# Linear attention and gated feed-forward on one core: where the output stage's sums and residual adds run

## The chip, the cores and the metric

The kernel runs on one core of one Trainium2 chip. A core has a matrix engine (TensorE, PE, with its weight load PEld), VectorE (DVE), ScalarE (ACT), GpSimd (POOL) and a queue that issues transfers (SyncE, SP). Engines run their own instruction streams in order and meet through semaphores. The metric is the device time of one execution in microseconds, as the median of several runs.

## The reference

One token block of 2048 x 1024 (bf16) goes through a linear-attention layer and a gated feed-forward layer, each behind a layer norm and with a residual:

```python
qkv = (x @ wqkv) ...                       # x: layernorm(A_x), 32 heads of 32
phi = lambda t: jnp.where(t > 0, t + 1, jnp.exp(t)) + 1e-6
kv = jnp.einsum("bhsd,bhse->bhde", phi(k), v)
z = jnp.einsum("bhsd->bhd", phi(k))
o = num / den                              # num = phi(q) kv, den = phi(q) z + 1e-6
h = x + o @ wo
gate, up = n @ W_gate, n @ W_up            # n: layernorm(h), F = 3584
out = h + (relu(gate) * up) @ W_down
```

## The kernel before

The 2048 tokens are 16 tiles `st` of 128. Most products are done in a seven-product form (P1 to P7) of a 2 x 2 block product instead of eight: it needs sums of weight blocks (`TW`) and of operand blocks (`S`), made ahead of the products, and additions to the results.

The program is a plan written out by hand: `PL.add` puts an operation at the end of its engine's list, and waits follow from what each operation reads and writes. So the order of the calls in the source is the order on each engine, SP's queue included. Buffers that share memory are named in `over` lists; the first write of the new one waits for the readers of the old.

The stages around the change, in order:

- *Query stage.* `q_group(r, ct)` runs eight groups of seven products, with hooks 1 to 7 between the products. VectorE forms phi with an add (L1170), a fast SBUF clamp (L915) and a combination (L918). In the second half (`r = 1`), `a2_num` and `a2_div` of the first tiles run too: `a2_num` is 32 small products into banks 0 to 3, and `a2_div` on VectorE divides (L1306, L1309, L1311, giving `o_st`) and sends the tile through a transposing transfer on SP (`T3d_st`) into one of six `oT` slots.
- *Single tiles.* For tiles 0 to 9, `a4_mm(st)` multiplies `oT(st)` by `wo` with 16 products into a bank pair, (4, 5) or (6, 7). `a4_h(st)` adds the residual tile `x2(st)` on VectorE (L1460; tile 9 in two halves, L1333) into one of three `hsb` slots and stores it. For tiles 0 to 7 ScalarE then takes statistics and normalizes (`a4_norm`), and a transposing transfer `T5d_st` puts the tile into `hnT`. Calls of `a2_num`/`a2_div` for the following tiles are put between the products by the table `at`; the table `aft` puts other work behind a tile.
- *Weight sums of wo.* `wo_sums` makes TWo1 to TWo4 on GpSimd in halves (two blocks of 512), the first two before tile 0, the others behind tiles 0 to 5.
- *Grouped tiles.* Tiles 10 to 15 go in three pairs through `o_group(p, ...)`, p = 5, 6, 7, of seven products each. `o_sums(p, i)` makes the four operand sums So of a pair: one on GpSimd, eleven on VectorE (L1363). ScalarE copies banks (`ofk1`, `ofk2`, `os7`, `osc`); the residual is added by GpSimd (`add_x`, L1406) to the copies, and VectorE adds the parts (L1412) or, in the third group, bank and residual (L1419). `store` sends a tile out through SP.
- *Feed-forward.* It starts with unit 0 on `hnT` (P1 of two blocks, banks 1 and 0, copied by ScalarE to banks 4 and 5). It needs the operand sums S1 to S4 (`s_sums`, L1544, VectorE), the weight sums of its first weights (`t_sums`, L1568; for this unit on GpSimd as eight 128x512 pieces, `pool_t`), and inner sums xs and g1 (L1624, L1602, VectorE).

Memory that matters: region RA holds the transposed input until the query stage ends, then the TWo sums (8 K columns), the So sums (4 K), and four residual tiles `x2a` (12 to 15). `xn` in region RXH (4 K) holds normalized tiles. `x2r` in region RE has three slots for residual tiles 8 to 10, and tile 11 reuses the first of them.

Of the kernel before, what the change touches and what calls it, by code (L numbers as in the profile page):

```python
# [132 lines left out]
def bass_sequential_preLN__linear_attn_block__glu_gated_reglu__prompt_kernel(  # L133
# [71 lines left out]
    with es:  # L205
# [21 lines left out]
        NX2 = 3  # L227
        NDIR = 10
        NXA = NST - TPP - NX2 - 1
# [59 lines left out]
        TWo = RA[:, 0:NDC * D].bitcast(f16).rearrange("p (j k c) -> p j k c", j=4, k=KH)  # L289
        So = RA[:, NDC * D:(NDC + 4) * D].bitcast(f16).rearrange("p (z i k t) -> p z i k t", z=2, i=4, k=KH)  # L290
        x2a = RA[:, (NDC + 4) * D:(NDC + 4 + NXA) * D].rearrange("p (a b) -> p a b", a=NXA)
        NXR = TPP + NX2 + 1

# [39 lines left out]
        xn = RXH[:, 0:NXN * D].rearrange("p (a b) -> p a b", a=NXN)  # L333
        hsb = RXH[:, NXN * D:(NXN + NHS) * D].rearrange("p (a b) -> p a b", a=NHS)
# [106 lines left out]
        B_TWo = bufs("TWo_", 4)  # L441
        B_Ef = bufs("Ef_", 2)
# [73 lines left out]
        ra_o = B_TWo + flat(B_So) + B_x2[TPP + NX2:]  # L516
        for b_ in ra_o:
            b_.over = flat(B_xnT)
        for b_ in B_x2[0:TPP]:
            b_.over = B_TWk  # L520
# [26 lines left out]
        for i, st in enumerate(range(NDIR, NST)):  # L547
            if i < NHS:
                j = st % NHS
                hp_home[st] = hsb[:, j, :]  # L550
                over = [B_hs[j]]
            else:
                hp_home[st] = xn[:, i - NHS, :]
                over = [B_xn[i - NHS]]
            for b_ in B_hp[st]:
                b_.over = over
        for b_ in B_D1:
            b_.over = B_xn + B_hs + [b for st in B_hp for b in B_hp[st]]
# [18 lines left out]
        for b_ in flat(B_hh) + B_out2:  # L577
            b_.over = flat(B_xnT) + flat(B_pqT) + ra_o
# [743 lines left out]
        def a4_mm(st, at):  # L1322
            k = st % NOT
            b = a4_bank[st] = min(H_PAIRS, key=lambda b: max(bank_last[b], bank_last[b + 1]))
            for nt in range(ND2):
                touch_bank(b + nt)
                for ct in range(NG):
                    for f_ in at.pop(nt * NG + ct, ()):
                        f_()
                    mm(bank(b + nt, NW), oT(st)[:, ct, :], wo[:, ct, nt * NW:(nt + 1) * NW],  # L1330
                       ct == 0, ct == NG - 1, [B_oT[k], B_wo[nt]], B_bank[b + nt], "a4_%d_%d" % (st, nt))
                if st == NDIR - 1:
                    PL.add("dve", lambda e, h=slice(nt * NW, (nt + 1) * NW), bk=b + nt: e.tensor_tensor(  # L1333
                        out=hsb[:, st % NHS, h], in0=bank(bk), in1=x2(st)[:, h], op=ALU.add),
                        reads=[B_bank[b + nt], B_x2[x2_slot(st)]], writes=[B_hs[st % NHS]], name="h_%d_%d" % (st, nt))

        def wo_sums(j, eng, k0, k1):
# [3 lines left out]
            def t(i):  # L1341
                return TWo[:, i, k0:k1, :], [B_TWo[i]]
# [4 lines left out]
                   reads=x[1] + y[1], writes=[B_TWo[j]], name="TWo%d" % (j + 1))  # L1347
# [18 lines left out]
        def o_group(p, bks, hooks, act_first):  # L1366
# [3 lines left out]
            s7, sc = (btmp[:, 1, :], B_bt[1]), (btmp[:, 0, :], B_bt[0])  # L1370
# [11 lines left out]
            def TW(j):  # L1382
                return (lambda kk: TWo[:, j, kk, :]), [B_TWo[j]]
# [16 lines left out]
            def res(st, h):  # L1400
                return x2(st)[:, h * NW:(h + 1) * NW], B_x2[x2_slot(st)]

            def add_x(src, st, h, dst=None):
                x, bx = res(st, h)
                d, db = src if dst is None else dst
                PL.add("pool", lambda e: e.tensor_tensor(out=d, in0=src[0], in1=x, op=ALU.add),  # L1406
                       reads=[bx] + ([] if dst is None else [src[1]]), writes=[db], name="ox_%d_%d" % (st, h))

            def fin(st, h, bk, s=None):
                d, db = half(st, h)  # L1410
                if s is not None:
                    PL.add("dve", lambda e: e.tensor_tensor(out=d, in0=bank(bk), in1=s[0], op=ALU.add),  # L1412
                           reads=[B_bank[bk], s[1]], writes=[db], name="h_%d_%d" % (st, h))
                elif act_first:
                    ident_act(Ef[:, h, :], bank(bk), [B_bank[bk]], [B_Ef[h]], "oc_%d_%d" % (st, h))
                    add_x((Ef[:, h, :], B_Ef[h]), st, h, (d, db))
                else:
                    x, bx = res(st, h)
                    PL.add("dve", lambda e: e.tensor_tensor(out=d, in0=bank(bk), in1=x, op=ALU.add),  # L1419
                           reads=[B_bank[bk], bx], writes=[db], name="h_%d_%d" % (st, h))  # L1420
# [5 lines left out]

            prod(a, X(0, 0), W(0, 0), True, "P1")
# [3 lines left out]
            ident_act(s7[0], bank(f), [B_bank[f]], [s7[1]], "os7")  # L1431
            add_x(s7, sb2, 0)
            hook(2)
            prod(b, SX(1), TW(1), False, "P6")
            ident_act(bank(c), bank(b), [B_bank[b]], [B_bank[c]], "ofk2")
            hook(3)
            prod(a, X(1, 0), W(1, 0), False, "P2")
            fin(sa, 0, a)
# [3 lines left out]
            add_x(sc, sb2, 1)  # L1442
            hook(5)
            prod(b, X(1, 1), TW(3), False, "P4")
            fin(sb2, 0, b, s7)
            hook(6)
            fin(sb2, 1, f, sc)
            store(sb2)
            prod(c, SX(3), W(1, 1), False, "P3")
            o_pend[1] = [lambda: fin(sa, 1, c), lambda: store(sa)]  # L1450
# [4 lines left out]
        def a4_h(st):  # L1455
# [3 lines left out]
            if st < NDIR - 1:  # L1459
# [3 lines left out]
            if TPP <= st and st + NX2 < NST:  # L1463
                if st + NX2 < NXR:
                    load_x2(st + NX2)
# [1175 lines left out]
```

## Time and profile before

| what | us |
|---|---|
| median of 3 runs (lowest, highest) | 722.0 (721.59, 722.17) |
| the profiled execution's own time | 722.16 |
| its span in the trace | 720.4 |
| PE busy | 703.7 (98%) |
| VectorE busy | 615.3 (85%) |
| ScalarE busy | 413.0 (57%) |
| GpSimd busy | 143.0 (20%) |
| DMA, 16 engines, queue q1 | 66.5% of the span |

The times in the trace are microseconds from the start of its span; durations are busy times of single instructions. A matmul row carries several products; one 128x512 product takes about 0.22 us, four of them 0.87. Idle time in front of an instruction is given with what released it, for example a DVE line or a transfer. Where a wait was for several things, the trace names the last.

### The profile page before, as it was taken

The numbers are of one execution on the slowest core, as the hardware profiler recorded it, in microseconds if no ns is written. First come the engines' busy times: TensorE is split into PE (matmuls) and PEld (weight loads), VectorE is DVE, ScalarE is ACT, GpSimd is POOL, SyncE is SP. The second block draws the span as 40 slices with busy tenths as digits, with TensorE's granted clock in tenths as the row PEclk, the third lists the DMA queues.
The fourth block names the chain that finished last, engine by engine and source line by source line (L and its number), as shares of the span: only waits on it lengthen the run. The fifth ranks groups of instructions, "written<-read, shape, count | busy, mean of one in ns | idle before, by whom it ended". The sixth has DMA issues, their size and how long they took to land.

```text
span 720.4 us, 13204 instructions
## 1 busy us (share of the span) xinstructions
PE 703.7 (98%) x4984; PEld 392.3 (54%) x5039; DVE 615.3 (85%) x978; ACT 413.0 (57%) x745; POOL 143.0 (20%) x197
## 2 busy tenths in 40 slices
PE   8999999999898999999999999999999999999998
PEld 4434444444443444555554568875555555547887
DVE  6978867899888889999999787878898888988885
ACT  4977667764853668787877402036766666643010
POOL 3221100004878322132313002220000000000331
PEclk9999999999999999999999999999999999999999
DMA  9852344015997799999997999995443534267996
GB/s 300 255 105 73 44 133 161 2 30 97 218 186 219 243 319 313 306 268 293 274 296 223 261 276 300 306 267 135 117 132 103 160 92 137 87 195 249 317 326 186
DMA packets 195104, 144.21 MB, mean 200 GB/s; under 512 B 53984, under 2 KB 172512, under 8 KB 195040
## 3 DMA queue, kind: packets, MB, share of 16 engines
q1 hardware_dynamic: 190048, 138.77, 66.5%
q0 software_dynamic: 4032, 3.67, 3.6%
q8 instruction: 40, 0.66, 0.4%
q10 hardware_dynamic: 960, 0.92, 0.4%
q14 instruction: 24, 0.20, 0.1%
HBM read 98.76 MB, written 32.51 MB: 182 GB/s over the span
## 4 chain that ended last, share of the span: by engine, by line
PE 81%; DVE 11%; issue 3%; DMA 2%; POOL 2%; ACT 1%; SPq 0%; DVEq 0%; POOLq 0%
PE ps L831 81%; DVE RE L1311 1%; DVE RX L915 1%; DVE RAB L918 1%; DVE RO L1568 1%; DMA RE<-RE 1%; POOL RX L1406 1%; DVE RW L767 1%; DMA RAB<-RXH 1%; DVE RXH L1460 1%; DVE RC L1054 0%; DVE RAB L1702 0%; POOL RXH L1406 0%; DMA RAB<-in_A_x_dram 0%; DVE rden L1309 0%
## 5 line engine op out<-in xcount | busy, mean ns | idle before, releaser
L836 ACT ACTIVATE ps<-ps 128x512 f32<-128x512 f32 (+1 forms) x263 | 133.0, 517 | 181.2 <-PE ps L831 127.9
L831 PE MATMUL ps<-RC,RO 128*128 128x512 f16 x616 | 147.0, 369 | 0.0
L831 PEld LDWEIGHTS ps<-RC,RO 128*128 128x128 f16 x616 | 60.1, 98 | 53.1 <-ACT ps L836 1.4
L836 ACT ACTIVATE RE<-ps 128x512 f32<-128x512 f32 (+3 forms) x106 | 63.8, 627 | 30.9 <-PE ps L831 16.6
L831 PE MATMUL ps<-RC,RWG 128*128 128x512 f16 x320 | 80.8, 379 | 0.0
L831 PE MATMUL ps<-RH,RWG 128*128 128x512 bf16 (+1 forms) x347 | 77.6, 348 | 0.8 <-ACT ps L836 0.7
L1972 POOL DMA_DIRECT2D out_dram<-RX x20 | 17.9, 1232 | 271.2 <-DVE RX L1963 218.4
L831 PE MATMUL ps<-RAB 128*128 128x512 bf16 (+3 forms) x272 | 58.8, 352 | 3.0 <-DVE RE L1311 1.5
L831 PE MATMUL ps<-RH,RO 128*128 128x512 bf16 (+1 forms) x228 | 59.2, 379 | 1.5
L1702 DVE TENSOR_TENSOR RE<-ps,RE 128x1024 bf16<-128x1024 f32 (+1 forms) x42 | 44.0, 1047 | 18.0 <-PE ps L831 17.8
L831 PE MATMUL ps<-RW,RAB 128*128 128x256 f16 (+3 forms) x368 | 55.2, 302 | 1.1 <-ACT RX L836 0.8
L831 PEld LDWEIGHTS ps<-RH,RWG 128*128 128x128 bf16 x348 | 33.9, 98 | 36.2 <-ACT ps L836 1.4
L831 PEld LDWEIGHTS ps<-RC,RWG 128*128 128x128 bf16 (+1 forms) x320 | 30.0, 98 | 34.5 <-ACT ps L836 5.8
L831 PEld LDWEIGHTS ps<-RW,RAB 128*128 128x128 f16 (+1 forms) x374 | 36.4, 98 | 16.9 <-ACT RX L836 1.5
L1963 DVE TENSOR_TENSOR RE<-ps,RE 128x512 f32<-128x512 f32 x44 | 30.2, 686 | 14.4 <-PE ps L831 11.8
L836 ACT ACTIVATE RX<-ps 128x512 f32<-128x512 f32 (+1 forms) x47 | 27.5, 597 | 25.6 <-PE ps L831 20.5
L831 PEld LDWEIGHTS ps<-RAB 128*128 128x128 bf16 (+1 forms) x274 | 26.0, 98 | 28.3 <-ACT ps L836 3.2
L1714 ACT ACTIVATE RAB<-RAB 128x1024 bf16<-128x1024 bf16 x28 | 29.5, 1053 | 19.3 <-DVE RAB L1702 19.3
L1702 DVE TENSOR_TENSOR RAB<-ps,RE 128x1024 bf16<-128x1024 f32 x28 | 34.2, 1221 | 7.3 <-PE ps L831 4.6
L1702 DVE TENSOR_TENSOR RAB<-RAB,RE 128x1024 bf16<-128x1024 bf16 x56 | 37.2, 685 | 3.1 <-ACT RE L836 2.7
L1568 DVE TENSOR_TENSOR RO<-RWG 128x1024 f16<-128x1024 bf16 x54 | 39.4, 730 | 0.0
L831 PEld LDWEIGHTS ps<-RH,RO 128*128 128x128 f16 (+1 forms) x256 | 24.4, 98 | 24.6 <-ACT RX L836 1.5
(210 smaller groups left out, 1305.2 us busy)
## 6 DMA issues: line engine op xcount, KB each, us to landing
RWG<-in_B_W_gate_dram SPq DMA_DIRECT2D x28, 512.0 KB, 6.1
RWG<-in_B_W_up_dram SPq DMA_DIRECT2D x28, 512.0 KB, 5.0
RW<-l_scr SPq DMA_DIRECT2D x20, 448.0 KB, 5.9
RW<-in_B_W_down_dram SPq DMA_DIRECT2D x14, 512.0 KB, 6.4
t_scr<-RW SPq DMA_DIRECT2D x14, 512.0 KB, 4.2
l_scr<-RX SPq DMA_DIRECT2D x7, 1024.0 KB, 8.5
RE<-l_scr SPq DMA_DIRECT2D x15, 448.0 KB, 6.1
RW<-t_scr SPq DMA_DIRECT2D x13, 448.0 KB, 5.7
```

The source lines that it names most:

```text
L767: PL.add("dve", lambda e: e.tensor_tensor(out=out, in0=in0, in1=in1, op=ALU.subtract), reads=reads, writes=writes, name="WT_%d" % q)
L831: lambda e: e.matmul(out_ap, lhsT, rhs, start=start, stop=stop, skip_group_check=skip),
L836: PL.add("act", lambda e: e.activation(out=dst, in_=src, func=func), reads=reads, writes=writes, name=name)
L915: PL.add("dve", lambda e: e.tensor_scalar(out=Et[:, k, :], in0=Et[:, k, :], scalar1=1.0, scalar2=1e-6, op0=ALU.min, op1=ALU.add), reads=[] ...
L918: PL.add("dve", lambda e: e.scalar_tensor_tensor(out=dst_ap, in0=src, scalar=C1, in1=Et[:, k, :], op0=ALU.add, op1=ALU.max), reads=[src_bu ...
L1311: PL.add("dve", lambda e: e.tensor_tensor(out=osb[:, k, :].rearrange("p (g h e) -> p g h e", h=HPG, e=Dh), in0=nv[:, :, :, 0:Dh], in1=rden ...
L1406: PL.add("pool", lambda e: e.tensor_tensor(out=d, in0=src[0], in1=x, op=ALU.add), reads=[bx] + ([] if dst is None else [src[1]]), writes=[ ...
L1568: PL.add(eng, lambda e: e.tensor_tensor(out=tb(j, u), in0=f0(u), in1=f1(u), op=ALU.subtract), reads=[B_w[i + x] for x in r] + ([B_T[k + x] ...
L1702: PL.add("dve", lambda e: e.tensor_tensor(out=dst, in0=in0, in1=in1, op=op), reads=reads, writes=writes, name=name)
L1714: PL.add("act", lambda e: e.activation(out=d, in_=d, func=ACTF.Relu), reads=[], writes=db, name=name)
L1963: PL.add(eng, lambda e: e.tensor_tensor(out=dst, in0=in0, in1=in1, op=op), reads=reads, writes=writes, name=name)
L1972: PL.add("pool", lambda e: e.dma_start(dst, src, accum_op=ALU.add), reads=[bsrc], writes=[B_hscr[st]], slot=sl, name="acc_%d_%d" % (st, dh))
```

## The change

The output stage divides its work otherwise between VectorE, GpSimd and ScalarE.

- All twelve So sums are made by GpSimd; GpSimd no longer adds residuals.
- In `o_group`, VectorE adds the residual as it reads the bank: `os7` and `ofx` (bank f plus each half of tile `sb2`'s residual, into SBUF as fp32), the two halves of tile `sa` from their banks, `hp` (the copy `osc` plus `ofx`, both in SBUF) and the last half from its bank. The ScalarE copies `os7` and `oc` are gone.
- TWo3 and TWo1 are made in the query stage, one 512 block in each of its eight groups, at hook 5, each waiting for the operation before the last one planned on VectorE. TWo2 and TWo4 stay behind tiles 2 to 5. TWo1 and TWo3 live in `xn`'s place; the normalized tiles move to `xo` in RA.
- For tiles 8 and 9 ScalarE writes the residual into the bank pair before the products (`a4_pre`), the products add to it, and ScalarE copies the sum out in halves. `a4_pre` also chooses the bank pair of every single tile.
- `x2r` has four slots; tile 11's residual is loaded with the others instead of after tile 8.
- The places in `at`, `aft` and the groups' hooks change: the divisions of tiles 12 to 15 come earlier, T5d_5 to T5d_7 later, the loads of residual tiles 12 to 15 earlier, and the S sums are spread over the third group.
- The first writes of the feed-forward tiles wait only for what lies in their own place in RA.

```diff
-        NX2 = 3
+        NX2 = 4
...
+        def TWo(j):
+            return (TWo_x if j % 2 == 0 else TWo_a)[:, j // 2]
...
-            b = a4_bank[st] = min(H_PAIRS, key=lambda b: max(bank_last[b], bank_last[b + 1]))
+            b, pre = a4_bank[st], st >= TPP
...
-                       ct == 0, ct == NG - 1, [B_oT[k], B_wo[nt]], B_bank[b + nt], "a4_%d_%d" % (st, nt))
-                if st == NDIR - 1:
-                    PL.add("dve", lambda e, h=slice(nt * NW, (nt + 1) * NW), bk=b + nt: e.tensor_tensor(
-                        out=hsb[:, st % NHS, h], in0=bank(bk), in1=x2(st)[:, h], op=ALU.add),
...
+                       ct == 0 and not pre, ct == NG - 1, [B_oT[k], B_wo[nt]], B_bank[b + nt], "a4_%d_%d" % (st, nt),
+                       skip=pre)
+                if pre:
+                    hs, h = st % NHS, slice(nt * NW, (nt + 1) * NW)
+                    ident_act(hsb[:, hs, h], bank(b + nt), [B_bank[b + nt]], [B_hs[hs]], "h_%d_%d" % (st, nt))
+
+        def a4_pre(st):
+            b = a4_bank[st] = H_PAIRS[st % 2]
+            if st >= TPP:
+                ident_act(ps[:, b:b + 2, :], x2(st).rearrange("p (a c) -> p a c", a=2), [B_x2[x2_slot(st)]],
+                          [B_bank[b], B_bank[b + 1]], "hx_%d" % st)
...
             prod(f, SX(2), TW(2), True, "P7")
-            ident_act(s7[0], bank(f), [B_bank[f]], [s7[1]], "os7")
-            add_x(s7, sb2, 0)
+            fin(s7, f, res(sb2, 0), "os7_%d" % p)
...
             ident_act(bank(c), bank(b), [B_bank[b]], [B_bank[c]], "ofk2")
+            fin(fx, f, res(sb2, 1), "ofx_%d" % p)
...
-            fin(sa, 0, a)
+            fin(half(sa, 0), a, res(sa, 0), "h_%d_0" % sa)
...
-            add_x(sc, sb2, 1)
+            fin(half(sb2, 1), [sc[0], [sc[1]]], (fx[0], [fx[1]]), "hp_%d_1" % sb2, fin_eng)
             hook(5)
             prod(b, X(1, 1), TW(3), False, "P4")
-            fin(sb2, 0, b, s7)
+            fin(half(sb2, 0), b, (s7[0], [s7[1]]), "h_%d_0" % sb2)
+            store(sb2)
...
+                hooks[5] = lambda i=r * (NG // 2) + ct: wo_sums((2, 0)[i // KH], "pool", i % KH, i % KH + 1,
+                                                               PL.prog["dve"][-2:-1])
...
-              6: {5: [nd]}, 7: {3: [nd]}, 8: {2: [nd, t5(4)]}, 9: {2: [nd, t5(5)]}}
-        aft = {0: [tw(2, 0)], 1: [tw(2, 2)], 2: [tw(1, 0)], 3: [tw(1, 2)], 4: [tw(3, 0)], 5: [tw(3, 2)],
-               8: sums(p0, (2, "pool")), 9: sums(p0, (0, "dve"), (1, "dve"), (3, "dve"))}
+              6: {5: [nd]}, 7: {3: [nd]}, 8: {1: [nd, t5(4)], 14: [nd, ldx(13), ldx(12)]}, 9: {11: [nd]}}
+        aft = {2: [tw(1, 0)], 3: [tw(1, 2)], 4: [tw(3, 0)], 5: [tw(3, 2)], 6: [pt, pt],
+               7: sums(p0, (2, "pool"), (0, "pool")), 8: sums(p0, (1, "pool"), (3, "pool")) + [pt]}
...
         o_group(p0, [4, 6, 5, 7], {
-            2: [nd], 4: sums(p0 + 1, (2, "dve"), (0, "dve")), 5: [nd, lambda: load_x2(13), lambda: load_x2(12)],
-            6: sums(p0 + 1, (1, "dve"), (3, "dve")) + [t5(6), t5(7)]}, True)
+            1: [nd, t5(5), t5(6)], 6: [t5(7), ldx(15), ldx(14)],
+            4: sums(p0 + 1, (2, "pool"), (0, "pool"), (1, "pool"), (3, "pool"))}, "dve")
...
-            1: [lambda: run(pool_t, 1)], 2: sums(p0 + 2, (2, "dve"), (0, "dve"), (1, "dve"), (3, "dve")),
-            3: [lambda: run(pool_t, 1), lambda: load_x2(15), lambda: load_x2(14)], 6: [ss[0], ss[1]]}, True)
+            2: sums(p0 + 2, (2, "pool"), (0, "pool"), (1, "pool"), (3, "pool")), 6: [pt]}, "dve")
...
-        o_group(p0 + 2, [4, 6, 5, 7], {2: [ss[2]], 4: [ss[3]]}, False)
+        o_group(p0 + 2, [4, 6, 5, 7], {1: [pt, ss[0]], 2: [pt], 3: [ss[1]], 5: [ss[2]], 7: [ss[3]]}, "dve")
```

## The prediction

> **What bounds the kernel now.** I read the page first: PE is busy 703.7 us of a span of 720.4, so only 16.7 us can be won without taking matmuls away. The stretches of the trace say where those microseconds lie (columns: stretch, its length, busy time of each engine, granted clock, DMA share, GB/s).
>
> ```profile
> core 0: us, PE busy (x) PEld busy (x) DVE busy (x) ACT busy (x) POOL busy (x), PEclk, DMA share, GB/s
> 148.00:182.40 34.40, 32.35 (x327) 13.97 (x331) 33.03 (x59) 19.61 (x34) 9.96 (x12) 1.00 0.42 78
> 182.40:206.00 23.60, 23.13 (x316) 10.91 (x322) 19.80 (x28) 20.95 (x31) 19.57 (x31) 1.00 1.02 223
> 206.00:238.40 32.40, 27.13 (x181) 11.10 (x182) 28.26 (x37) 12.93 (x23) 23.89 (x18) 1.00 0.78 194
> 238.40:460.00 221.60, 220.68 (x1257) 124.39 (x1275) 194.08 (x259) 134.20 (x229) 47.08 (x68) 1.00 0.97 283
> ```
>
> The three grouped pairs of tiles (206 to 238) leave PE 5.27 us idle, the end of the query stage 2.05; the feed-forward stage after it has PE busy 99.6%. The clock is 1.00 everywhere, so it explains nothing. Next, what ended PE's idle times from 145 to 240 us (total, times, longest):
>
> ```profile
> PE ps L831 <- DVE RE L1311: 3.3, 2, 1.8
> PE ps L831 <- ACT ps L836: 1.9, 3, 1.0
> PE ps L831 <- ACT RX L836: 0.8, 1, 0.8
> PE ps L831 <- DVE RAB L1602: 0.8, 1, 0.8
> PE ps L831 <- DVE RAB L1363: 0.2, 1, 0.2
> ```
>
> L1311 is `o_st`, the division that frees the four banks of the next `a2_num`. Why VectorE is late there is seen by setting its timeline beside GpSimd's (start, duration).
>
> ```profile
> 173.69 0.28 DVE L915 TENSOR_SCALAR RX<-RX 128x512 bf16<-128x512 bf16 x1
> ...
> 177.57 2.21 DVE L915 TENSOR_SCALAR RX<-RX 128x512 bf16<-128x512 bf16 x1
> ...
> 187.08 1.23 DVE L1311 TENSOR_TENSOR RE<-ps,rden 128x1024 bf16<-128x1024 f32 x1
> ```
>
> ```profile
> 177.51 2.12 POOL L1346 TENSOR_TENSOR RAB<-RW 128x1024 f16<-128x1024 bf16 x1
> ...
> 187.20 2.13 POOL L1346 TENSOR_TENSOR RAB<-RW,RAB 128x1024 f16<-128x1024 bf16 x1
> ...
> 229.06 2.13 POOL L1406 TENSOR_TENSOR RXH<-RX,RAB 128x512 bf16<-128x512 f32 x1
> ```
>
> The same L915 takes 0.28 alone and 2.21 when it starts 0.06 after a GpSimd weight sum: it stands until that ends. An L1311, which reads PSUM, takes its usual 1.23 beside another weight sum, and the weight sum its usual 2.13. So the two engines block each other only in VectorE's fast SBUF forms. In the groups it is the same: POOL's 128x512 adds take 1.15 alone and 2.13 beside VectorE's S sums, which take 1.57 to 2.06. At 233.32 VectorE then waits 1.04 for such an add:
>
> ```profile
> 226.01 2.06 DVE L1544 TENSOR_TENSOR RC<-RC,RH 128x2048 f16<-128x2048 f16 x1
> ...
> 233.32 0.69 DVE L1412 TENSOR_TENSOR RXH<-ps,RX 128x512 bf16<-128x512 f32 x1 [1.04 <-POOL RX L1406]
> ```
>
> **Part 1, weight sums into the query stage.** Four GpSimd sums of 2.12 (TWo3, TWo1) leave 165 to 184 us. They held L915 twice: 1.05 instead of 0.28 at 169.06 and 2.21 instead of 0.28 at 177.57, together 2.7 us of VectorE. The chain from there to L1311 at 181.12 has no VectorE idle time worth naming, so `o_6` ends at 182.35 - 2.7 = 179.7. PE wants `num_7` at 182.40 - 1.84 = 180.56: the 1.84 goes, 0.9 us to spare. What is late next is no longer VectorE: `h_2` would end at 181.0, and a4_4, which needs its bank pair, starts at 183.79 - 1.84 = 181.95.
> Against that stand eight new sums of one 512 block, 1.15 each by POOL's L1363 at 206.16. Each is tied to the VectorE operation two before, an L918, and runs beside the two L1170 that follow; they read PSUM and last 1.28 together (133.33). L915 comes 1.38 after the first of them starts (134.71): cover 1.28 to 1.38 against 1.15 plus about 0.1 of hand-over. Cost taken: 0. Without that cover each holds an L915 for up to 1.15: in the first half VectorE's idle time (0.95 before L915 in each group) takes nearly all of it, in the second, with none, four would cost 4.6 of VectorE. Wo was loaded at 100.5, so no transfer is waited for. Term: -1.84, from 0 to -1.84 kept as bounds.
>
> **Part 2, residual of tiles 8 and 9 in PSUM by ScalarE.** VectorE loses `h_8` (1.23) and the two `h_9` halves (1.37 with their idle). ScalarE gains two 128x1024 writes into PSUM that no row shows: 1.05 by L1714 (128x1024 from SBUF, 1.06), 1.16 as twice the ps<-ps 128x512 (0.58); I take 1.05. Also four 128x512 copies of 0.6, 0.5 apart. ScalarE is already busy 20.95 of 23.60 here. By its rows (statistics 2.23, norm 1.13 a tile) from `h_2` at 181.1: hx_8 ends 196.1, wanted at 197.5; hx_9 ends 200.5, wanted 201.7; h_9_1 ends 207.0. Behind it stands the first group's copy ofk1, 207.0 to 207.6, which P6 waits for; PE reaches P6 at 207.7. Cost 0.15, from 0 to 1.1.
> One `num` more falls into these tiles (+0.31) and one fewer into the groups: 0. PE ends a4_9 at 206.98 - 1.84 + 0.31 = 205.45.
>
> **Part 3, pair sums on GpSimd, VectorE on PSUM.** From 206 to 238 VectorE loses eleven So sums (9.1 us busy by L1363's rows, where 0.43 each unblocked would be 4.7, and 1.9 of waiting for T3d transposes in front of them) and gains ten 128x512 operations at 0.62: net about -3. Seven of the ten read PSUM (0.68 by L1412); three (`hp`) add two fp32 tiles in SBUF, which no row shows: 0.43 (L1363 alone) to 1.33 (L1363 blocked), taken 0.68. GpSimd gets twelve sums at 1.15 = 13.8 and loses ten adds `ox` (14.9); ScalarE loses seven copies of 0.6. Each group needs its four within a PE time of 7 x 0.87 = 6.1 us, 4.6 are asked. By the rows: of the first group 204.1 to 208.7 (So3, the first made, is wanted at 206.9, So2, the third made, at 207.7), of the second 209.8 to 214.4 (wanted 213.1 and 213.95), of the third 214.6 to 219.2 (wanted 219.2 and 220.1). T3d_13 leaves at 203.2, and with the 5.71 us of the transpose at 206.48 it lands at 208.9; T3d_15 leaves at 208.9, lands 214.6. The loads of tiles 12 and 13 are issued at 204.5 rather than 218.09, tiles 14 and 15 at 215.5; wanted 214 and 220. On SP the stores of tiles 8 and 9 now wait for ScalarE (205.0, 207.0) with T3d_14 and T3d_15 queued behind them; these wait for `o_14` (206.4) and `o_15` (208.9) anyway: 0. T5d_5 and T5d_6 go behind T3d_15 (209), T5d_7 behind the store of tile 11, to 214; S1 is the first to need them, at 219. The weight load that followed them goes to about 216, and the next behind the store of tile 13 to 219; before, they were issued at 222.43 and 229.09, so both are earlier. Tile 11's load moves to 123.5, behind the three of its kind: 0.
>
> So PE's 23.34 us from 206.98 to 230.32 becomes 21 x 0.87 + 0.31 + 0.25 (num_15 on `o_15`'s predecessor 0.1, P6 0.15) = 18.8: feed-forward begins at 205.45 + 18.8 = 224.3, 6.0 earlier than 230.32.
> [...]
>
> **Part 4, start of the feed-forward stage.** PE idles 0.74 and 0.76 there and reaches the product that waits for L1602 6.6 us of work after its start: 230.9. VectorE now has in a row S1, two residual adds, S2, h, hp, S3, h, S4, h, four xs and g1: with before's contended rows 1.57 + 1.2 + 2.0 + 1.2 + 1.5 + 0.6 + 1.55 + 0.6 + 2.3 + 0.42 = 12.95 from 219.05 (`h_12_1` done): 232.0. With uncontended rows (S 1.15) it is 229. I take the contended, five GpSimd T sums being still there. PE waits 1.1 instead of 1.5: -0.4. The rest of the kernel moves along.
>
> **Sum.** -1.53 to the end of a4_9 (part 1's 1.84 less the `num` that comes early), -4.54 in the groups (23.34 to 18.8), -0.4 at the feed-forward stage: 6.4 off the profiled execution's 722.16 (span 720.4 and 1.76 around it), 715.8; the median of the runs, 722.0, is 0.16 lower: 715.6, put at 715.7.
>
> **Rivals.**
> *Late VectorE at the feed-forward stage.* T5d_7 stands on SP behind the store of tile 11, which waits for `h_11_0` at 213.4. If it lands 5.7 after its issue at 215, S1 starts at 220.7 and everything behind it 1.65 later: 717.3. For: transposes of 5.7 in this window; against: T5d's median of 3.9.
> *ScalarE becomes the bound.* If its chain is 1.5 us later than summed, hx_9 and ofk1 hold PE by 0.3 and 1.5: 717.5. For: 25.4 us asked of 23.5 to 207; against: both have a microsecond.
> *Given back.* DMA is 97% busy from 238 to 460; if weights arrive at fixed times the 6.4 come back as waits: 722.0. Against: PE idles 0.92 there now, and loads are started by freed buffers.
> *Slower: GpSimd becomes the bound.* If So sums run at the 2.13 of L1406 instead of 1.15, thirteen operations from 204.1 end at 231.8, feed-forward starts at 232.7, 2.4 later than now, less the 0.4 of part 4: 722.0 + 2.0 = 724.0. It decides from 1.95 us a sum. For: 2.13 four times in 224 to 231; against: each stood beside S sums, and beside PSUM-reading VectorE GpSimd kept its time.
>
> **Chances.** Main case 0.55 (own range 714.2 to 717.0), late VectorE 0.22, ScalarE 0.10, given back 0.06, GpSimd 0.07. The range takes in the first three, and on top of 717.5 part 2's upper cost (1.1) and the loss of half of part 1 (0.9): 714.2 to 719.5. About 0.2% (1.4 us) can be told from no change: faster 0.87, same 0.06, slower 0.07.
>
> **What would show it.** L915 near 0.3 all through 150 to 180 and no PE wait before `num_7`; So sums at 1.15; the first feed-forward product (RH,RWG) near 224.3; L1602 near 232 with about a microsecond of PE idle. Wrong if L915 grows in the query stage, if PE waits for So sums or for ScalarE near 201 and 207, or if PE idle shows up after 240.

## The result, and the profile after

| | before | after |
|---|---|---|
| median of 5 runs (lowest, highest), us | 721.59 (720.4, 722.17) | 716.94 (716.61, 718.54) |
| span of the profiled execution | 720.4 | 715.5 |
| its own time | 722.16 | 717.18 |
| VectorE busy in the span | 615.3 | 608.7 |
| GpSimd busy | 143.0 | 144.1 |

The ratio of the times is 0.9942, 95% interval 0.9927 to 0.9957: the changed kernel is faster, by 0.6%, which is clear of the noise. PE is busy 703.6 us, as before; what went is PE's idle time. In the new line numbers, PE is L845, ScalarE's copy L850, the clamp L929, the adds of the query stage L1184, the division L1325, TWo L1366, So L1383, the groups' additions L1422, S L1548, T L1572.

The stretches of the changed kernel, cut at `num_7`, the end of tile 9, the start of the feed-forward stage and the product that takes g1 (columns as before: stretch, length, busy time of PE, PEld, DVE, ACT, POOL, clock, DMA share, GB/s):

```profile
core 0: us, PE busy (x) PEld busy (x) DVE busy (x) ACT busy (x) POOL busy (x), PEclk, DMA share, GB/s
145.00:180.33 35.33, 35.12 (x370) 15.28 (x373) 33.57 (x63) 21.01 (x37) 6.93 (x11) 1.00 0.37 71
180.33:205.33 25.00, 24.28 (x353) 11.46 (x358) 19.29 (x29) 23.95 (x36) 20.34 (x34) 1.00 1.04 212
205.33:225.53 20.20, 18.97 (x115) 7.76 (x116) 16.10 (x20) 6.81 (x12) 19.21 (x16) 1.00 1.08 244
225.53:233.46 7.93, 6.54 (x32) 2.77 (x30) 7.86 (x13) 2.87 (x6) 2.66 (x2) 1.00 0.42 135
233.46:460.00 226.54, 225.65 (x1304) 128.83 (x1321) 199.28 (x265) 135.34 (x231) 46.95 (x68) 1.00 0.97 284
```

The end of the query stage has almost no idle time of PE left (0.21 of 35.33). In the groups GpSimd is now busy 19.21 of 20.20 us, and PE is idle 1.23 of them. Before, PE was idle 3.74 of the 23.34 us of the same stretch:

```profile
206.98:214.90 7.92, 7.65 (x95) 3.33 (x95) 6.70 (x11) 2.96 (x5) 5.05 (x5) 1.00 0.98 197
214.90:223.10 8.20, 6.54 (x30) 2.51 (x29) 6.84 (x11) 3.35 (x6) 4.34 (x4) 1.00 0.68 152
223.10:230.32 7.22, 5.41 (x26) 2.11 (x24) 7.19 (x7) 2.75 (x5) 7.22 (x5) 1.00 0.82 262
```

From the 64 small `RE` products near 121 us to the product that takes g1, the two traces differ by 4.80 us: 1.91 less up to `num_7`, 0.42 more from there to the end of tile 9 (one `num` more stands there now), 3.14 less in the groups and 0.17 less at the start of the feed-forward stage.

Which waits were in the groups before shows where the 3.14 come from: PE's idle time there fell by 2.51, and of the rest 0.31 is the `num` that moved. PE waited 3.67 there, by the trace's list, and 2.66 of it stood behind So sums on VectorE. The longest wait (1.49) was for the division of tile 15, which VectorE began only behind two So sums, themselves late by a transfer; the four sums of this form waited 1.9 for transfers and took 1.10 on average, where others take 0.42 unblocked; the next (0.96) was for a bank copy behind a VectorE addition that stood behind four more So sums. 0.21 was a So sum itself, 0.84 stood behind an S sum, and 0.17 was a ScalarE copy. First the row of these four sums (busy time, mean ns of one, idle time before them and what ended it), then the two waits:

```profile
L1363 DVE TENSOR_TENSOR RAB<-RE 128x512 f16<-128x512 bf16 x4 | 4.2, 1097 | 1.9 <-DMA RE<-RE 1.9
```

```profile
216.67 1.04 PE L831 MATMUL ps<-RAB 128*128 128x512 f16 x4 [1.49 <-DVE RE L1311]
...
225.15 1.04 PE L831 MATMUL ps<-RAB 128*128 128x512 f16 x4 [0.96 <-ACT ps L836]
```

None of these waits is in the changed kernel. What ended PE's idle times from 145 to 240 us (total, times, longest):

```profile
PE ps L845 <- ACT ps L850: 2.2, 2, 1.4
PE ps L845 <- issue: 0.3, 2, 0.2
PE ps L845 <- DVE RE L1325: 0.3, 1, 0.3
```

The 1.84 us in front of `num_7` are gone. Two waits for ScalarE copies are left: 0.84 in the groups, 1.39 in the feed-forward stage. In the query stage the timeline shows a new sum beside the two adds that read PSUM:

```profile
152.28 0.68 DVE L1184 TENSOR_TENSOR RX<-ps,RX 128x512 f32<-128x512 f32 x1
...
152.51 1.16 POOL L1366 TENSOR_TENSOR RXH<-RW 128x512 f16<-128x512 bf16 x1 [5.68 <-DVE RAB L932]
152.88 0.68 DVE L1184 TENSOR_TENSOR RXH<-ps,RXH 128x512 f32<-128x512 f32 x1
...
153.66 0.29 DVE L929 TENSOR_SCALAR RX<-RX 128x512 bf16<-128x512 bf16 x1
```

The sum ends at 153.67 as the clamp begins; sum, adds and clamp all last what they last alone (1.15 for the sum at 206.16 in the kernel before, 0.68, 0.29). All eight sums take 1.16; of the clamps one grew, at 128.40, from 0.29 to 0.45.

The 0.84 in the groups is read from the same view, over four engines:

```profile
205.02 2.35 SPq L641 DMA_TRANSPOSE RE<-RE  x1
207.55 0.92 SPq L637 DMA_DIRECT2D RAB<-in_A_x_dram  x2
208.52 0.43 SPq L637 DMA_DIRECT2D out_dram<-RXH  x1
...
212.44 1.20 DVE L1422 TENSOR_TENSOR RXH<-RX 128x512 bf16<-128x512 f32 x1 [1.37 <-DMA out_dram<-RXH]
...
214.28 0.58 ACT L850 ACTIVATE ps<-ps 128x512 f32<-128x512 f32 x1 [3.03 <-DVE RXH L1422]
...
214.91 1.04 PE L845 MATMUL ps<-RAB 128*128 128x512 f16 x4 [0.84 <-ACT ps L850]
```

`hp` of tile 11 writes the `hsb` slot from which tile 8 is stored. `hp` is the addition of two fp32 tiles in SBUF that finishes a half of the pair's second tile. The store stands on SP behind the issue of T3d_13 (2.35) and the loads of two residual tiles; it leaves at 208.52, and VectorE waits 1.37 for its landing. Bank 5, copy `ofk1` and P6 of the next pair are late behind it. At the start of the feed-forward stage:

```profile
220.31 2.10 DVE L1548 TENSOR_TENSOR RC<-RH 128x2048 f16<-128x2048 bf16 x1
221.28 3.26 POOL L1572 TENSOR_TENSOR RO<-RWG 128x512 f16<-128x512 bf16 x2
223.53 2.09 DVE L1548 TENSOR_TENSOR RC<-RC,RH 128x2048 f16<-128x2048 f16 x1
224.49 3.69 POOL L1572 TENSOR_TENSOR RO<-RWG,RO 128x512 f16<-128x512 bf16 x2
227.10 2.17 DVE L1548 TENSOR_TENSOR RC<-RH 128x2048 f16<-128x2048 bf16 x1
229.19 0.68 DVE L1422 TENSOR_TENSOR RAB<-ps,RX 128x512 bf16<-128x512 f32 x1
229.79 1.21 DVE L1548 TENSOR_TENSOR RC<-RH,RC 128x2048 f16<-128x2048 bf16 x1
...
229.90 0.58 ACT L850 ACTIVATE ps<-ps 128x512 f32<-128x512 f32 x1 [2.67 <-DVE RAB L1422]
...
230.54 1.04 PE L845 MATMUL ps<-RH,RWG 128*128 128x512 bf16 x4 [1.39 <-ACT ps L850]
```

S sums take 2.1 beside GpSimd's T sums and 1.21 without (the last). `h_15_0` (229.19) stands behind S3, the copy out of its bank behind it, and PE behind the copy.

### The profile page after: what moved, and what is told of

Read it like the earlier page. It is cut to its first block, busy times and chain, and to the rows that moved or that the text cites. A ratio compares the mean times of both kernels' runs of the same rounds, so it can differ in the third digit from the quotient of the medians.

```text
span 715.5 us, 13215 instructions
## 1 busy us (share of the span) xinstructions
PE 703.6 (98%) x4984; PEld 392.9 (55%) x5039; DVE 608.7 (85%) x974; ACT 413.1 (58%) x744; POOL 144.1 (20%) x202
## 3 DMA queue, kind: packets, MB, share of 16 engines
q0 software_dynamic: 4032, 3.67, 3.5%
## 4 chain that ended last, share of the span: by engine, by line
PE 91%; DVE 5%; issue 2%; ACT 1%; DMA 1%; DVEq 0%; ACTq 0%
PE ps L845 91%; DVE RC L1548 1%; DMA RAB<-RXH 1%; DVE RO L1572 1%; DVE RAB L1422 0%; DVE RAB L1706 0%; ACT RXH L885 0%; DMA RE<-in_A_x_dram 0%; DVE RW L781 0%; ACT ps L850 0%; ACT RX L850 0%; DVE RWG L1093 0%; PE ps L1006 0%; DVE ps L1706 0%; DVE RE L1967 0%
## 5 line engine op out<-in xcount | busy, mean ns | idle before, releaser
L850 ACT ACTIVATE ps<-ps 128x512 f32<-128x512 f32 (+1 forms) x263 | 133.1, 517 | 180.4 <-PE ps L845 127.6
L845 PE MATMUL ps<-RC,RO 128*128 128x512 f16 x616 | 147.0, 369 | 0.0
L845 PEld LDWEIGHTS ps<-RC,RO 128*128 128x128 f16 x616 | 60.1, 98 | 53.1 <-ACT ps L850 1.2
L850 ACT ACTIVATE RE<-ps 128x512 f32<-128x512 f32 (+3 forms) x106 | 63.8, 627 | 31.7 <-PE ps L845 17.6
L845 PE MATMUL ps<-RC,RWG 128*128 128x512 f16 x320 | 80.8, 379 | 0.0
L845 PE MATMUL ps<-RH,RWG 128*128 128x512 bf16 (+1 forms) x347 | 77.6, 348 | 1.4 <-ACT ps L850 1.4
L845 PE MATMUL ps<-RH,RO 128*128 128x512 bf16 (+1 forms) x228 | 59.2, 379 | 1.5
L845 PE MATMUL ps<-RW,RAB 128*128 128x256 f16 (+3 forms) x370 | 55.6, 303 | 0.2
L845 PEld LDWEIGHTS ps<-RH,RWG 128*128 128x128 bf16 x348 | 33.9, 98 | 36.9 <-ACT ps L850 2.0
L845 PE MATMUL ps<-RAB 128*128 128x512 bf16 (+3 forms) x248 | 52.6, 349 | 1.1 <-ACT ps L850 0.8
L845 PEld LDWEIGHTS ps<-RC,RWG 128*128 128x128 bf16 (+1 forms) x320 | 30.0, 98 | 34.4 <-ACT ps L850 5.8
L845 PEld LDWEIGHTS ps<-RW,RAB 128*128 128x128 f16 (+1 forms) x374 | 36.3, 98 | 16.2 <-ACT RX L850 1.1
L1572 DVE TENSOR_TENSOR RO<-RWG 128x1024 f16<-128x1024 bf16 x54 | 39.4, 729 | 0.0
L850 ACT ACTIVATE RX<-ps 128x512 f32<-128x512 f32 (+1 forms) x40 | 23.5, 597 | 25.9 <-PE ps L845 22.7
L1572 DVE TENSOR_TENSOR RO<-RWG,RO 128x1024 f16<-128x1024 bf16 x54 | 38.2, 708 | 0.0
L845 PEld LDWEIGHTS ps<-RH,RO 128*128 128x128 f16 (+1 forms) x256 | 24.4, 98 | 24.6 <-ACT RX L850 1.5
```

Source lines behind the costliest of these rows:

```text
L845: lambda e: e.matmul(out_ap, lhsT, rhs, start=start, stop=stop, skip_group_check=skip),
L850: PL.add("act", lambda e: e.activation(out=dst, in_=src, func=func), reads=reads, writes=writes, name=name)
L1572: PL.add(eng, lambda e: e.tensor_tensor(out=tb(j, u), in0=f0(u), in1=f1(u), op=ALU.subtract), reads=[B_w[i + x] for x in r] + ([B_T[k + x] ...
```

## The experiments

The experiments run with a stand-in: each transposing transfer is replaced by two plain transfers of half a tile each, so tiles arrive untransposed and the results are not those of the reference. Both kernels were run in this form first, and all others are edits of the changed one.

```diff
-            return PL.add("sp", lambda e: e.dma_start_transpose(dst_ap, src_ap), ...
+                e.dma_start(v(dst_ap, 0), v(src_ap, 0)).then_inc(slot.sem, 16)
+                return e.dma_start(v(dst_ap, 1), v(src_ap, 1))
```

Profiled executions differ by up to 0.8 us ahead of 121 us, where their work is the same but for the transfers. So besides the median, the table measures in each trace from one common mark, the 64 small `RE` products near 121 us, to `num_15`, from there to the feed-forward stage, and from there to the g1 product. In the two kernels of before `num_15` stands later in the program, so only their sums compare with the other rows. The last columns are PE's longest wait from 145 to 245 us and the mean clock of each run.

| kernel | median | to num_15 | to feed-forward | to g1 | sum | longest wait | mean clock |
|---|---|---|---|---|---|---|---|
| before (real transfers) | 721.59 | 90.90 | 18.20 | 8.10 | 117.20 | 1.84 | profile 1.000 |
| after (real transfers) | 716.94 | 85.58 | 18.89 | 7.93 | 112.40 | 1.39 | 5 at 1.000 |
| before, stand-in | 722.1 | 90.94 | 17.46 | 8.10 | 116.50 | 1.8 | 10 at 1.000, 2 at 0.998 |
| after, stand-in | 716.5 | 85.58 | 17.92 | 8.37 | 111.87 | 1.83 | 5 at 1.000, 1 at 0.998 |
| sums behind the tiles | 721.48 | 90.28 | 17.93 | 8.37 | 116.58 | 2.13 | 11 at 0.998 |
| half of them behind | 718.65 | 87.28 | 17.92 | 8.56 | 113.76 | 2.0 | 3 at 1.000, 0.999, 0.998 |
| sums beside the clamp | 719.01 | 87.95 | 17.93 | 8.36 | 114.24 | 1.8 | 5 at 1.000 |
| residual on VectorE | 716.41 | 85.75 | 17.93 | 7.98 | 111.66 | 1.4 | 4 at 1.000, 1 at 0.999 |
| So on VectorE | 720.67 | 85.60 | 24.65 | 6.26 | 116.51 | 3.9 | 5 at 0.995, 5 at 0.998, 1 at 1.000 |
| five So a pair | 719.18 | 85.59 | 20.30 | 8.41 | 114.30 | 1.23 | 5 at 1.000 |
| T3, T4 on VectorE | 714.62 | 85.60 | 17.93 | 6.26 | 109.79 | 0.3 | 5 at 1.000 |
| late store | 716.91 | 85.59 | 17.91 | 8.39 | 111.89 | 1.85 | 5 at 1.000 |
| late store, T3, T4 on VectorE | 715.44 | 85.58 | 19.03 | 6.26 | 110.87 | 0.85 | 5 at 1.000 |

**The two kernels with the stand-in transfers.**

> Stand-in for the kernel before: each transposing transfer is replaced by two plain transfers of half a tile each in 256 byte pieces, so that tiles arrive untransposed; every engine's instructions and all waits stay. It is the base for the experiments. Expected: within 1% of 721.6 us, with the same waits as the kernel before (PE 1.8 for num_7, about 4 in the groups, 1.5 at the start of feed-forward); the wait for the transfer of tile 13 (PE 1.5, by L1311) may be shorter if plain transfers land sooner.

> The same stand-in for the changed kernel. Expected if the gain comes from the engines and not from transposing transfers: 4 to 6 us less than the stand-in of before, PE idle of about 1.4 at the start of feed-forward again, 0 to 0.9 in the second group (the store of tile 8, 3.9 us after its issue, may be earlier). Rival: if half of the gain came from transposing transfers that no longer queue in front of one another, the difference shrinks to 2 to 3 us.

They stand 5.6 apart in the medians and 4.63 by the marks, where the real ones stand 4.65 and 4.80: the stand-in keeps the effect. Two things it does not keep. In the kernel before, the longest wait in the groups (1.49, for a division) is 0.5 here, and the one of 0.84 for a ScalarE copy is 1.7. In the changed kernel the store of tile 8 now leaves at 206.57, `hp` of tile 11 doesn't wait for it, and the stretch from `num_15` to the feed-forward stage takes 0.97 less than in the real changed kernel. Of this 0.44 are given back by a longer wait behind them.

**Part 1 undone: TWo1 and TWo3 as GpSimd sums of two blocks before and behind the first tiles.**

```diff
-                hooks[5] = lambda i=r * (NG // 2) + ct: wo_sums((2, 0)[i // KH], "pool", i % KH, i % KH + 1, ...
...
-        aft = {2: [tw(1, 0)], ...
+        aft = {0: [tw(2, 0)], 1: [tw(2, 2)], 2: [tw(1, 0)], ...
+        for k_ in (0, 2):
+            wo_sums(0, "pool", k_, k_ + 2, PL.prog["pe"][-1:])
```

> The changed stand-in with part 1 undone: TWo1 and TWo3 again as four GpSimd sums of 2.1 us, two from the end of the query stage on, one each behind tiles 0 and 1; all else as changed. Theory (a GpSimd sum holds VectorE's fast SBUF clamp): two of the clamps between 167 and 178 us grow from 0.28 to 1 to 2.2, the division of tile 6 ends 2 to 2.7 us later than its 179.3, PE waits 1.2 to 1.8 for num_7, and the kernel is 1.3 to 1.9 us slower than the changed stand-in (716.5). Rival (the gain is made in the groups, lateness before them is absorbed by the waits there): within 0.4 us of it.

It costs 5.0 by the medians (721.48 against 716.5) and 4.70 by the marks, far more than the theory expected. Two clamps are held here for 2.14 and 2.20; the kernel before had one half and one whole hold (1.05 and 2.21). The second one, and what comes of it, in the timeline:

```profile
178.33 2.12 POOL L1373 TENSOR_TENSOR RXH<-RW 128x1024 f16<-128x1024 bf16 x1
...
178.40 2.20 DVE L936 TENSOR_SCALAR RX<-RX 128x512 bf16<-128x512 bf16 x1
...
183.22 0.37 PE L852 MATMUL ps<-kvz,RAB 32*128 32x33 bf16 x32 [2.13 <-DVE RE L1332]
183.52 1.83 PE L852 MATMUL ps<-RW,RE 128*128 128x512 bf16 x5
185.15 3.04 PE L852 MATMUL ps<-RW,RX 128*128 128x512 bf16 x8
```

Eight products take 3.04 here instead of the usual 1.89. The stretches of one microsecond each say why (the column behind POOL is the granted clock):

```profile
182.00:183.00 1.00, 0.00 (x0) 0.00 (x0) 1.00 (x1) 0.00 (x0) 0.90 (x3) 1.00 0.02 6
183.00:184.00 1.00, 0.78 (x35) 0.52 (x36) 1.00 (x2) 0.00 (x0) 1.00 (x1) 1.00 0.63 138
184.00:185.00 1.00, 1.00 (x4) 0.37 (x3) 0.86 (x4) 0.67 (x1) 0.48 (x1) 0.53 0.63 138
185.00:186.00 1.00, 1.00 (x3) 0.30 (x2) 1.00 (x1) 0.97 (x3) 0.31 (x1) 0.50 0.68 164
186.00:187.00 1.00, 1.00 (x4) 0.45 (x3) 1.00 (x2) 1.00 (x3) 0.19 (x1) 0.50 1.10 328
187.00:188.00 1.00, 1.00 (x5) 0.36 (x4) 0.24 (x1) 1.00 (x2) 0.82 (x4) 0.77 1.27 308
```

After a PE wait of 2.13 the clock is granted at half for about 3.5 us. The four last rows lose 0.47 + 0.50 + 0.50 + 0.23 = 1.70 us. The marks say the same: from `num_7` to `num_8` this kernel takes 5.12 us where the changed stand-in takes 3.43, 1.69 more. Up to `num_7` it is 3.01 late, by PE waits of 0.32, 0.22 and 2.13 in the main, and behind `num_8` nothing more is lost up to `num_15`: 3.01 + 1.69 = 4.70. This is read from the one profiled execution; all 11 executions had the same mean clock of 0.998.

**Half of part 1 undone, to separate waits from clock.** As above, but TWo1 stays in the query stage (`if r == 1:` in front of the hook), so that only one clamp is held.

> Half of part 1 undone: TWo3 (two GpSimd sums of 2.12) goes back behind tiles 0 and 1 of the output stage, TWo1 stays in the query stage. One clamp is then held for about 2.1 instead of two. Theory (a hold costs what is left after 0.9 us of slack; the rest of the 5.0 us that both sums cost was the clock, granted at 0.50 for 3.7 us after a PE wait of 2.13): PE waits 1.0 to 1.3 before num_7, the clock stays at 1.00, 717.5 to 717.9. Rival (the 5.0 us are a price of the sums, in proportion): 719.0.

By the marks 1.89, by the median 2.15: between the two, nearer to the rival's number. The trace takes the theory's side on the clock: the clamp is held 2.20, PE waits 1.41 before `num_7`, and the clock stays at 1.00. It stays there behind a later wait of 2.03 too. What was wrong is the slack: a hold 1.91 longer than the clamp alone gave a wait of 1.41, so it is 0.5 us, not 0.9. Of the other 0.5 by the marks, 0.2 lies ahead of 165 us, before the hold, and 0.2 behind the start of the feed-forward stage, where PE waits 2.03 instead of 1.83.

**The cover taken away: sums start behind the second add, beside the clamp.**

```diff
-                    hooks[6] = lambda t=ct: a2_num(t)
-                hooks[5] = ... PL.prog["dve"][-2:-1])
+                hooks[6] = lambda i=r * (NG // 2) + ct, num=num: (num(), wo_sums(..., PL.prog["dve"][-1:]))
```

> The eight weight sums of the query stage stay there, but each starts behind the second of the two adds that read PSUM rather than beside the first, so it runs beside the clamp of the normal map (RX<-RX), which works in SBUF alone. Theory (the cover is what makes them free): the clamp beside them grows from 0.28 to about 1.1, VectorE comes some 3 us late to the last division of the stage, 0.6 to 0.9 of which is its slack, PE waits 2.2 to 2.4 before num_7: 718.7 if the granted clock stays at 1.00, about 720.6 if it falls to 0.50 for some 3.7 us after that wait, as it did after a wait of 2.13 in the kernel with the sums behind the tiles. Rival (VectorE's idle time takes it): 716.5.

The median is 2.5 above, the marks 2.37, as the theory said, but not where it said. The sum starts just after the clamp, and the combination behind the clamp is held instead, 1.52 where it otherwise takes 0.69:

```profile
154.17 0.29 DVE L936 TENSOR_SCALAR RX<-RX 128x512 bf16<-128x512 bf16 x1
154.22 1.25 POOL L1373 TENSOR_TENSOR RXH<-RW 128x512 f16<-128x512 bf16 x1 [6.42 <-DVE RXH L1191]
154.50 1.52 DVE L939 SCALAR_TENSOR_TENSOR RAB<-RX 128x512 bf16<-128x512 f32 x1
...
157.63 0.60 PE L852 MATMUL ps<-RWG,RH 128*128 128x512 f16 x2 [0.56 <-ACT ps L857]
```

PE waits twice 0.32 and twice 0.56 between 155 and 166 us (1.76 of the 2.37), and not at all at `num_7`; the rest of the 2.37 is lost in the same two groups. The combination takes 0.69 alone where the clamp takes 0.28 for a tile of the same size, and yet it is held too. In all six rows of this run with 1.52 or 1.53 both its inputs are in SBUF. No row shows the combination with an input in PSUM begun behind a sum; the second add of the query stage, which reads PSUM, does begin behind one and takes its usual 0.68 (at 152.88 above).

**Part 2 undone: tiles 8 and 9 get their residual from VectorE again.** `pre` is set to False, `hx` is left out, and the additions of before are back.

> The changed stand-in with part 2 undone: for tiles 8 and 9 VectorE adds the residual to the banks again (1.22, and two halves of 0.68), ScalarE writes no residual into PSUM and copies no halves. Theory (part 2 keeps VectorE in time for the divisions that were moved forward): the divisions of tiles 13 to 15 end 1.2 to 2.6 us later, PE waits 1 to 2 us for num_14 and num_15, of which the wait of 1.83 at the start of feed-forward takes nothing since VectorE is late by as much: 1 to 2 us slower than the changed stand-in. Rival (VectorE's idle time there, 0.8 to 1.5 before each division, absorbs it): within 0.3 us, or 0.3 faster since ScalarE's bank copy comes earlier.

716.41 against 716.5, and 0.21 less by the marks: the theory's 1 to 2 us don't come, VectorE's idle time takes the work as the rival said, and part 2 is worth nothing measurable here.

**Part 3 undone for two groups: the four So sums of groups 2 and 3 on VectorE.**

```diff
-            4: sums(p0 + 1, (2, "pool"), (0, "pool"), (1, "pool"), (3, "pool"))}, "dve")
+            4: sums(p0 + 1, (2, "dve"), (0, "dve"), (1, "dve"), (3, "dve"))}, "dve")
```

and the same for `p0 + 2`.

> The changed stand-in with the eight pair sums of the second and third group made by VectorE at the same places of the program (the four of the first stay on GpSimd). Theory (VectorE is the engine in short supply from the groups to the start of feed-forward, and GpSimd's 1.15 a sum is free): VectorE gets 8 x 0.43 = 3.4 us more, or up to 8 us where GpSimd's weight sums hold it; the banks of the groups come free later and the S sums end 2 to 4 us later, 2 to 4 us slower than the changed stand-in. Rival (the holding is what costs, and GpSimd with 9.2 us less to do has its weight sums done before the S sums, which then run at 1.2): within 0.5 us, or faster by up to 1.

4.2 by the median, a little above the theory. The four sums of the second pair stand beside GpSimd's T sums, which now run earlier, and take 1.25 each, where 0.42 is measured for those of the third; a bank comes free late, PE waits 3.85 at once, and from 218 to 224 the clock is granted at 0.50 to 0.54, which loses 2.9. Together that is about the 6.73 more in the groups; 2.11 come back behind them, where the S sums find GpSimd done and take 1.22. So the run prices the sums on VectorE beside these T sums, not by themselves. The other pieces of part 3, the residual adds taken from GpSimd and the ScalarE copies left out, and the earlier divisions and loads, were undone in no run; how much of the 3.14 us of the groups each would bring by itself is open.

**One sum more for each pair: how much room GpSimd has.**

```diff
-            return [lambda i=i, e=e: o_sums(p, i, e) for i, e in what]
+            return [lambda i=i, e=e: o_sums(p, i, e) for i, e in (what[:1] if what[0][0] == 2 else ()) + what]
```

> The first pair sum of each grouped pair of tiles is made twice by GpSimd (five sums a pair instead of four, 15 instead of 12), the results are the same. Theory (GpSimd has slack in the groups: five sums at 1.15 to 1.2 are 5.8 to 6.1 us against 6.4 us of PE time a pair): the twelve-sum chain that ends at 220.2 ends near 222, PE waits at most 0.5: 716.5 to 717.0. Rival (GpSimd's chain already is the bound of the groups, as its sums run almost without a gap from 203.8 to 220.2): three sums more cost 3 x 1.15 = 3.5 less two gaps of 1.1 and 0.45, 1.9 or more: 718.4 to 720.

The rival was right: 719.18, 2.43 by the marks. PE waits 0.70 and 1.23 for So sums that had no wait in front of them before, the first of them here:

```profile
208.71 1.15 POOL L1390 TENSOR_TENSOR RAB<-RX,RAB 128x512 f16<-128x512 bf16 x1
208.78 1.02 PE L852 MATMUL ps<-RAB 128*128 128x512 f16 x4 [0.70 <-POOL RAB L1390]
```

**The T sums that hold the S sums: T3 and T4 of unit 0 on VectorE, behind g1.**

```diff
-        pool_t = t_sums(0, "pool")
+        pool_t = t_sums(0, "pool")[0:4]
...
+                    t3 = t_sums(0)[2:4] if p_ == 0 else []
+                if q == 0:
+                    pre += t3
```

> The changed stand-in, but the last four of GpSimd's eight weight sums of unit 0 (T3 and T4) are made by VectorE in two instructions of 128x1024 behind g1, where it has 2.3 us idle. Theory (the S sums stand still for GpSimd's sums): S2, the hp after it and S3 fall from 2.09, 1.04, 2.17 to about 1.2, 0.7, 1.2; the last half of tile 15 is ready 2.2 us sooner, the PE wait of 1.83 at the start of feed-forward goes, the kernel is 1.4 to 1.8 us faster than the changed stand-in (716.5). Rival (VectorE's sheer amount of work bounds, not the holding): PE waits at the inner products instead, time within 0.3 us or slower.

714.62, 1.9 less than the changed kernel in the same form (2.08 by the marks), a little more than the theory's 1.4 to 1.8. S2 and S3 fall from 2.09 and 2.17 to 1.21, which S4 took already:

```profile
222.41 1.21 DVE L1555 TENSOR_TENSOR RC<-RC,RH 128x2048 f16<-128x2048 f16 x1
...
224.74 1.21 DVE L1555 TENSOR_TENSOR RC<-RH 128x2048 f16<-128x2048 bf16 x1
```

PE has 0.6 us of waits left from 145 to 245 us. This edit beats both kernels, as far as the stand-in tells.

**The late store put back, in both versions.** Tile 8's store is issued behind tile 9's.

> The store of tile 8 is issued behind that of tile 9, some 2.5 us later, so its buffer comes free late for the hp sum of tile 11, as it did in the changed kernel with its transposing transfers. Theory: hp of tile 11 starts 1.4 to 1.9 later than 210.8, the last product chain of the group (P6 of the next pair, through bank 5 and a ScalarE copy) waits 0.8 to 1.3, the feed-forward stage starts that much later; about 0.4 of it is given back there, because PE waits less for VectorE's sums: 716.9 to 717.4. Rival (the group has room, the wait is not on the path): 716.5.

> The same late store in the kernel whose T3 and T4 weight sums are made by VectorE behind g1 (714.62 without the late store). Theory: the wait of 0.8 to 1.3 at P6 is the same and nothing is given back at the feed-forward stage, where no wait is left to absorb it: 715.4 to 715.9. Rival (some other wait behind it takes it up): 714.6.

Without the T edit: 716.91, 0.4 more by the medians, at the lower end of the theory, but only 0.02 by the marks. The profiled execution of this kernel met a wait of `hp` of only 0.65 and no wait at P6, so neither the mechanism nor a cost is shown here. With the T edit: 715.44, 0.8 more, 1.08 by the marks, with every one of the five executions above those without the late store (715.11 at least, against 714.99 at most). The wait is there, and nothing is given back:

```profile
211.51 1.61 DVE L1429 TENSOR_TENSOR RXH<-RX 128x512 bf16<-128x512 f32 x1 [0.96 <-DMA out_dram<-RXH]
...
214.39 1.04 PE L852 MATMUL ps<-RAB 128*128 128x512 f16 x4 [0.85 <-ACT ps L857]
```

## Why the prediction was right, and where its steps were off

The forecast was 715.7 and the time is 716.94, inside the range and just inside the main case's own (to 717.0); of the 6.3 us forecast 4.65 came. By the number alone the rival of a late VectorE (717.3) is nearer, so the traces have to decide, and they show the mechanism as told, with one wait more than forecast. From the common mark on, part 1 was put at -1.84 and gave -1.91, the `num` that comes early at +0.31 and gave +0.42, the groups at -4.54 and gave -3.14, the start of the feed-forward stage at -0.40 and gave -0.17. In the trace the sum fell short by 1.5 us of span (715.5, where 715.8 - 1.76 = 714.0 was worked out): 1.4 of it in the groups, 0.2 at the start of the feed-forward stage, and 0.1 the other way before them.

| step | predicted | measured |
|---|---|---|
| end of tile 9 | 205.45 | 205.33 |
| groups | 18.8 | 20.20 |
| start of feed-forward | 224.3 | 225.53 |
| PE wait there | 1.1 | 1.39 |
| hx, each | 1.05 | 1.03, 1.00 |
| So sum | 1.15 | 1.15 to 1.48 |
| hp | 0.68 (0.43 to 1.33) | 0.69 to 1.20 |
| VectorE's row S1 to g1 | 12.95, from 219.05 | 13.1, from 220.31 |

*Part 1* held: the wait before `num_7` is gone, and the eight sums (1.16 each) are hidden by the adds that read PSUM (0.68 each). The price named for lost cover was right in kind: 2.4 us, shown by starting the sums 1.2 us later, though it came through the combination and not through the clamp. The 0.9 us to spare were 0.5. (The two `h_9` halves of part 2's working are 1.37 without their idle time, and 1.61 with it; no term rests on it.)

*Part 2* held as a cost of nothing, and ScalarE's chain ended at 206.99 where 207.0 was worked out.

*Part 3* is where the step failed. The text put the stores of tiles 8 and 9 at 0, since what is queued behind them on SP waits for something later anyway. It asked who is queued behind the stores, but not who waits for the store to land: `hp` of tile 11 takes over its buffer. The store left at 208.52, `hp` waited 1.37, P6 0.84. Two things made it late: T3d_13 went at 205.02, not 203.2, as T3d_12 (202.19) and T5d_4 (203.54) were still being issued ahead of it, and its own issue held SP for 2.35. What it costs, the late store with T3 and T4 on VectorE showed: 1.08 by the marks, with nothing behind it to give anything back. In the changed kernel itself the wait is 0.84, and against the stand-in, which doesn't have it, 0.97 - 0.44 = 0.53 are left at the g1 product. Another buffer for tile 11, which would take the wait away, was not measured. The rest of the 1.4 is PE's wait of 0.28 in front of `num_15` for the division of tile 14, put at 0.1, and 0.4 more of busy time than 21 x 0.87 + 0.31 gives.

The room that GpSimd has in the groups was overrated. "4.6 us asked of 6.1" compares whole pairs; the working's own rows had the third sum of the first pair at about 207.6 for a product that wants it at 207.7. The five-sum kernel gave GpSimd 3 x 1.15 = 3.45 us more, and 2.43 came out as time, so by an estimate the room in all three pairs is about 1.0 us. By this run the slower rival would have taken the whole gain (4.63) at 4.63 + 1.0 = 5.6 us more over twelve sums, an estimated 1.6 us a sum and not 1.95. Ten of the twelve sums did run at 1.15, beside VectorE's PSUM reads as argued, or, for the one at 211.94, beside an `hp` that grew instead (1.20); this is what kept that rival off. The other two (1.46 and 1.48) ran beside `hp`.

*Part 4*: the row's length was right; it began 1.26 late, as it stands behind the late group. The PE wait came one link earlier than told, at a ScalarE copy behind `h_15_0`, not at g1. Taking before's contended rows was the right choice: the S sums took 2.1 beside T sums, and 1.21 without. The T3, T4 run shows that this contention is the cause of PE's wait there, and that 1.9 us lay in it in the stand-in.

*Rivals.* VectorE late by T5d_7: VectorE was late by 1.26, but S1 (220.31) follows `h_12_1` without a wait for a transfer; the late group made it late. ScalarE as the bound: no. Given back later: no, from the g1 product to the end of the span it is 482.0 us in both kernels.

Undoing part 1 (+5.0) and part of part 3 (+4.2) together cost more than the whole change gained. The gains aren't a sum of parts: each undoing puts a PE wait above 2 us in place (2.13 and 3.85), which costs itself, and then the clock stood near half for some us, 1.70 and 2.9 us of time.

## What to carry to other kernels

Before a sum is moved to GpSimd, look what VectorE does in those microseconds: beside adds that read PSUM it was free here (sums of 1.16, adds of 0.68 as alone), beside the clamp, the combination with two SBUF inputs, `hp` and the S sums it was not: VectorE's clamp went from 0.28 to as much as 2.20, its combination from 0.69 to 1.52, its S sum from 1.21 to 2.17, `hp` from 0.68 to 1.20 in the changed kernel, GpSimd's So sum from 1.15 to as much as 1.48. When a transfer moves on a queue, ask not only who is queued behind it but who takes over its buffer, and when it lands. A wait of the matrix engine isn't always worth its own length alone: one of 2.13 also cost some 3.5 us at half clock here, 1.7 us of time, where one of 2.03 in another profiled execution cost nothing more.

## What the runs showed of the hardware that was not expected

The clock. The kernel before, run 55 times beside the experiments (a 56th execution, of 1500.68 us, is left out), had a mean clock of 1.000 in 38 executions (median 722.2) and of 0.998 in 17 (median 724.0); its longest PE wait in the profile is 1.84. The changed kernel with T3 and T4 on VectorE, longest wait 0.3, had 1.000 in all of 5; the kernel with a wait of 2.13 had 0.998 in all of 11. The removed wait may thus also have taken out a half-clock stretch that struck some executions. This isn't shown: none of those was profiled, five executions would all be at 1.000 by chance about one time in six (0.69 to the fifth power), and the late-start and late-store kernels, with longest waits of 1.82 and 1.85, had 1.000 in all of 5 too.

What is held. The prediction read from its rows that the two engines block each other only in VectorE's fast SBUF forms, such as the clamp, 0.28 alone. But the combination with two SBUF inputs, 0.69 alone, grew to 1.52 beside a sum, and the fp32 addition `hp`, 0.68 with GpSimd idle (T3 and T4 on VectorE), to 1.20 beside a So sum in the changed kernel and to as much as 1.61 in the late-store kernel with T3 and T4 on VectorE; the line was drawn too narrowly. Why the engines hold each other in these operations, no run shows.
